# Fewer and larger on-chip transposes, casting loads from Pool's queue, and chunk extremes by trees, in a chunk-selecting attention with a gated feed-forward

## The chip, the core and the metric

The kernel runs on one core of one Trainium2 chip. The metric is the device time of one execution in microseconds (us). The profile's span of the same execution is about 2 us shorter than its device time. On one core an execution counts as fast unless it is over 1.5% above the fastest of the same kernel.

## The reference

There are 4 batches, 8 heads, 768 positions and 64 values per head. For each query the attention picks 6 of 24 chunks of 32 keys, by an upper bound made from each chunk's smallest and largest key, and attends only to those, causally. What comes out goes through a gated feed-forward layer of 512 to 1,536 to 512.

```python
k_chunks = k.reshape(B, H, nc, 32, D)
k_min, k_max = np.min(k_chunks, axis=3), np.max(k_chunks, axis=3)
ub = sum over d of maximum(q * k_min, q * k_max)      # one bound for each query and chunk
ub = np.where(causal, ub, -1e9)
top_chunks = np.argsort(ub, axis=-1)[..., -6:]
attn = softmax(scale * q @ k^T, only in top_chunks and causal) @ v
x = attn, heads side by side                           # (3072, 512)
out = (sigmoid(x @ w_gate) * (x @ w_val)) @ w_out
```

## The kernel before

The work is cut into eight units: batch 0 to 3, and the first (a) or second (b) 384 query rows. Unit 2b is the second half of batch 2. While TensorE computes the scores of one unit, the feed-forward of the unit before it is mixed in, and so is the preparation of the unit after it. Each engine's instructions stand in a fixed list; where an input came late, the engine stood in front of that instruction, and what was listed behind it waited too.

Data that needs its axes swapped is transposed by DMA, issued by SyncE. `hk` holds keys with the head dimension on the partitions, `hq` holds queries in the same way, with 32 rows below that mark chunks that were not selected, and `xT` holds the attention output for the feed-forward. Each of these is sent in pieces of one block of 128 rows:

```python
def keys_wide(u):                         # 3 transposes for each unit, 8 heads each
    nc.gpsimd.tensor_copy(kn16[u.half][:, :, :, 0:D], u.k)          # fp32 -> fp16
    for x in range(HB):                                              # HB = 3
        r = T * u.half + 128 * x
        nc.sync.dma_start_transpose(headK[u.b % 2][:, :, r:r + 128],
                                    kn16[u.half][:, x].rearrange("p h c -> p (h c)"))

def send_rows(u, j, x):                   # 6 for each unit, 4 heads each
    nc.sync.dma_start_transpose(headQ[u.half][:, 4 * j:4 * j + 4, 128 * x:128 * x + 128],
                                qn16[:, x, 4 * j:4 * j + 4].rearrange("p h c -> p (h c)"))

def turn(u, c):                           # 4 for each unit, 3 blocks each
    ...
    nc.sync.dma_start_transpose(u.xT[:, c, :].rearrange("p (x i) -> p x i", x=HB),
                                u.x[:, c].rearrange("p x d -> p (x d)"))
```

For each batch, chunk extremes come from a second load of the keys, in two spans of four heads (`kc`, 96 partitions = 4 heads x 24 chunks). VectorE reduces a strided view:

```python
def span_reduce(u, j, e):                 # e = 0: max, e = 1: min
    src = u.kc[j].rearrange("p s d -> p d s")
    for d0 in (0, 32):
        nc.vector.tensor_reduce(out=u.kmm[:, e, d0:d0 + 32], in_=src[:, d0:d0 + 32],
                                op=(ALU.max, ALU.min)[e], axis=AX.X)
```

Key, query and value blocks are loaded as fp32 by SyncE, and Pool casts keys and values to fp16 (`keys_wide` above, `cast_v`). Units 0a and 0b are prepared another way, in an opening that is written out by hand (`opening`).

The softmax here doesn't subtract the row's maximum and nothing guards it: scores larger than these inputs give would overflow.

Of the kernel before, what the change touches and what calls it, by code (L numbers as in the profile page):

```python
# [18 lines left out]
def kernel(  # L19
# [25 lines left out]
    loads = ctx.enter_context(tc.tile_pool(name="loads", bufs=2))  # L45
    kcp = ctx.enter_context(tc.tile_pool(name="kcp", bufs=1))
    loadv = ctx.enter_context(tc.tile_pool(name="loadv", bufs=1))
    sel = ctx.enter_context(tc.tile_pool(name="sel", bufs=1))
    ubp = ctx.enter_context(tc.tile_pool(name="ubp", bufs=2))
    attp = ctx.enter_context(tc.tile_pool(name="attp", bufs=3))  # L50
# [4 lines left out]
    hglp = ctx.enter_context(tc.tile_pool(name="hglp", bufs=15))  # L55
# [41 lines left out]
    def load_v(u):  # L97
        u.v = loadv.tile([128, HB, H, D], F32, tag="v", name=f"v_{u.name}")
        for i in range(HB):
            r = T * u.half + 128 * i  # L100
            nc.sync.dma_start(u.v[:, i], v[u.b, :, r:r + 128].rearrange("h p d -> p h d"))
# [6 lines left out]
    def load_block(u, n, i):  # L108
        src = {"k": k, "q": q, "v": v}[n]
        if i == 0:  # L110
            pool = loadv if n == "v" else loads
            tag = n if n == "v" else "raw" + n
            setattr(u, n, pool.tile([128, HB, H, D], F32, tag=tag, name=f"raw{n}_{u.name}"))
        r = T * u.half + 128 * i
        nc.sync.dma_start(getattr(u, n)[:, i], src[u.b, :, r:r + 128].rearrange("h p d -> p h d"))
# [5 lines left out]
    def load(u):  # L121
        for n, src in (("k", k), ("q", q)):
            t = loads.tile([128, H, HB, D], F32, tag="raw" + n, name=f"raw{n}_{u.name}")
# [6 lines left out]
    def regroup(u, n, parts):  # L130
        raw = getattr(u, "raw" + n)
        if not hasattr(u, n):
            setattr(u, n, (kn16[0] if n == "k" else qn16).bitcast(F32))
# [12 lines left out]
    qn16 = keep.tile([128, HB, H, 128], F16, tag="qn", name="qn")  # L146
    for i in range(2):
        kcat.append(keep.tile([128, H, 32], F32, tag=f"kcat{i}", name=f"kcat{i}"))
        headK.append(keep.tile([128, H, S], F16, tag=f"hk{i}", name=f"hk{i}"))
        kn16.append(keep.tile([128, HB, H, 128], F16, tag=f"kn{i}", name=f"kn{i}"))  # L150
        headQ.append(keep.tile([128, H, T], F16, tag=f"hq{i}", name=f"hq{i}"))
# [3 lines left out]
    def fill_pattern(i, eng):  # L155
        eng.dma_start(headK[i][64:96],
                      epat.rearrange("p c s -> p (c s)").unsqueeze(1).to_broadcast([32, H, S]))

    def constants():
# [6 lines left out]
        fill_pattern(0, nc.sync)  # L166
# [16 lines left out]
        nc.vector.memset(headQ[0][64:96, :, 0:128], 0.0)  # L183
        nc.vector.tensor_copy(ident16, ident32)

    def pattern_rows():
# [4 lines left out]
        nc.gpsimd.memset(qn16[:, :, :, 64:128], 0.0)  # L191
# [43 lines left out]
    def keys_f(u, p, eng):  # L235
        ps = u.kps.pop(p)
        for e in range(2):
            eng(headK[u.b % 2][0:64, 2 * p + e, u.rows], ps[64 * e:64 * e + 64])
# [34 lines left out]
    def queries_f(u, p, eng):  # L273
        ps = u.qps.pop(p)
        for e in range(2):
            eng(headQ[u.half][0:64, 2 * p + e, :], ps[64 * e:64 * e + 64])

    def keys_wide(u):
        nc.gpsimd.tensor_copy(kn16[u.half][:, :, :, 0:D], u.k)
        for x in range(HB):  # L280
            r = T * u.half + 128 * x
            nc.sync.dma_start_transpose(headK[u.b % 2][:, :, r:r + 128],
                                        kn16[u.half][:, x].rearrange("p h c -> p (h c)"))

    def span_reduce(u, j, e):
        if e == 0:
            u.kmm = sel.tile([96, 2, D], F32, tag="kmm", name=f"kmm_{u.name}_{j}")
        src = u.kc[j].rearrange("p s d -> p d s")
        for d0 in (0, 32):
            nc.vector.tensor_reduce(out=u.kmm[:, e, d0:d0 + 32], in_=src[:, d0:d0 + 32],  # L290
                                    op=(ALU.max, ALU.min)[e], axis=AX.X)
# [8 lines left out]
    def queries_wide(u):  # L300
        nc.gpsimd.tensor_copy(qn16[:, :, :, 0:D], u.q)
        if u.sel0:
            nc.gpsimd.memset(qn16[:, 0, :, 64:96], 0.0)
            first_rows(u, 0)

    def first_rows(u, x):
        for j in range(2):
            send_rows(u, j, x)

    def send_rows(u, j, x):  # L310
        nc.sync.dma_start_transpose(headQ[u.half][:, 4 * j:4 * j + 4, 128 * x:128 * x + 128],  # L311
                                    qn16[:, x, 4 * j:4 * j + 4].rearrange("p h c -> p (h c)"))
# [389 lines left out]
```

## Time and profile before

| | before |
|---|---|
| device time, median | 402.75 us (400.92 to 404.79, 4 runs) |
| span of the profiled execution | 398.7 us |
| TensorE (PE) busy, idle | 324.7 us, 74.0 us |
| mean granted clock of TensorE | 0.906 |
| VectorE (DVE), ScalarE (ACT), Pool busy | 180.3, 207.9, 79.5 us |

These are lines of the page of the kernel before: its span, the busy time of each engine, and two rows that cut the span into 40 slices of 10 us. A digit of the PE row is the busy share in tenths, and of the PEclk row the granted TensorE clock in tenths.

```profile
span 398.7 us, 6796 instructions
PE 324.7 (81%) x2547; PEld 195.7 (49%) x2547; DVE 180.3 (45%) x472; ACT 207.9 (52%) x441; POOL 79.5 (20%) x116
...
PE   5672778968697888959959796878988995999996
...
PEclk9867999996889696979978999696999999899999
```

No engine is full. TensorE is the busiest, and the dips in its PE row are followed by dips of its clock. The Trainium skill, "TensorE: Matmul & The Clock Gate" (Part 1, "What's actually happening"), says that the clock is halved after an idle window of about 3.4 us and released after a busy one. The trace agrees on the length: its clock records show twelve stretches at half clock, ten of 6.8 us and two of 3.4 us, nearly all just after a gap. Together they are 75.1 us, and half of that over the span of 398.7 us gives the missing 0.094.

The next lines are TensorE's waits. Each names the tile and line that waited, the engine and tile that ended the wait, the sum in us, the number of waits, and the longest.

```profile
PE xps_0a L415 <- DVE xT_0a L416: 5.9, 1, 5.9
PE kmT_1a L295 <- DVE kmm_1a L290: 5.2, 1, 5.2
...
PE v_0b L429 <- DVE hg_0b L432: 4.0, 1, 4.0
PE g_1b L423 <- DMA xT_1b<-xnat_1b: 3.9, 1, 3.9
PE g_2a L423 <- DMA xT_2a<-xnat_2a: 3.6, 1, 3.6
...
PE g_3a L423 <- DMA xT_3a<-xnat_3a: 3.1, 1, 3.1
PE sc_1b L378 <- DMA hq<-qn: 2.7, 1, 2.7
```

There are two families. TensorE waits for VectorE, which reduces chunks (`kmm`) or does what stands behind the reductions (`hg`, `xT_0a`). And it waits for transposes, `xT` and `hq`. The cost of one reduction, and the landing time of one query-row transpose, are in a group line of the same page and in a line of the view of DMA issues (mean ns of one instruction; median us from issue to landing):

```profile
L290 DVE TENSOR_REDUCE kmm_1a<-kc_1a 96x32 f32<-96x1024 f32 x8 | 14.6, 1864 | 6.2 <-DMA kc_1a<-in_k_dram 6.2
...
hq<-qn SPq DMA_TRANSPOSE x36, 2.5
```

How the transposes queue up is seen in the timeline of SyncE's queue at the boundary between units 3a and 3b (start us, duration us, what; a row may join several instructions):

```profile
326.58 3.82 SPq L311 DMA_TRANSPOSE hq<-qn  x3
330.49 0.53 SPq L443 DMA_DIRECT2D out_dram<-osb_2b  x1
331.13 3.86 SPq L311 DMA_TRANSPOSE hq<-qn  x3
335.08 0.54 SPq L443 DMA_DIRECT2D out_dram<-osb_2b  x1
335.71 1.21 SPq L410 DMA_TRANSPOSE xT_3a<-xnat_3a  x1
```

Six query-row transposes, at 1.27 us of issue each, stand ahead of the last `xT` copy of the unit before. TensorE waits 3.1 us for it (`g_3a` above).

In the opening, VectorE's timeline shows reductions ahead of the work that TensorE needs:

```profile
31.77 3.63 DVE L290 TENSOR_REDUCE kmm_1a<-kc_1a 96x32 f32<-96x1024 f32 x2 [1.32 <-DMA kc_1a<-in_k_dram]
35.32 0.18 DVE L402 RECIPROCAL rz_0a<-pv_0a 128x6 f32<-128x6 f32 x1
35.42 1.81 DVE L290 TENSOR_REDUCE kmm_1a<-kc_1a 96x32 f32<-96x1024 f32 x1
37.16 0.54 DVE L404 TENSOR_TENSOR xnat_0a<-pv_0a,rz_0a 128x384 f16<-128x384 f32 x1
```

TensorE stands for 5.9 us until 38.0 (`xps_0a` in the waits).

### The profile page before, as it was taken

The page shows a single profiled execution, that of the slowest core. Times are in us where ns is not written, and L with a number is a line of the kernel's source. Part 1 is how long each engine was busy: PE and PEld are TensorE (multiplying, and loading weights), DVE is VectorE, ACT ScalarE, POOL GpSimd, SP SyncE. Part 2 cuts the span into 40 slices and gives each one's busy share as a digit, 9 for nine tenths or more (in the row PEclk, how much of TensorE's full clock was granted, in tenths as well). Part 3 has the DMA queues.
Part 4 walks back from the last instruction along what each step waited for, and adds up shares of the span by engine and source line. Part 5 has one row for each costly group of instructions (what it writes and reads, how often), then busy time and mean ns, then how long its engine had stood idle before and what let it go on. Part 6 is the DMA issues. An engine that isn't in the chain of part 4 may idle for free. (4 is left out here: it accounts for less than half of the span.)

```text
span 398.7 us, 6796 instructions
## 1 busy us (share of the span) xinstructions
PE 324.7 (81%) x2547; PEld 195.7 (49%) x2547; DVE 180.3 (45%) x472; ACT 207.9 (52%) x441; POOL 79.5 (20%) x116
## 2 busy tenths in 40 slices
PE   5672778968697888959959796878988995999996
PEld 3361435535354445736535453555555553665552
DVE  6588547354435650393303772356323541431330
ACT  3670457657754224737537534465747634676331
POOL 3393003810051003201050113110114111011000
PEclk9867999996889696979978999696999999899999
DMA  8999990598439846796255956494437015001002
GB/s 223 265 223 193 196 207 2 96 224 185 91 67 191 159 76 144 153 134 117 77 115 118 216 80 127 95 195 109 100 94 111 12 49 128 12 12 56 36 2 79
DMA packets 125633, 47.54 MB, mean 119 GB/s; under 512 B 112992, under 2 KB 121952, under 8 KB 125024
## 3 DMA queue, kind: packets, MB, share of 16 engines
q1 hardware_dynamic: 120848, 42.39, 52.0%
q0 software_dynamic: 4752, 4.72, 7.0%
q8 instruction: 20, 0.33, 0.4%
q14 instruction: 13, 0.11, 0.1%
HBM read 33.03 MB, written 6.29 MB: 99 GB/s over the span
## 5 line engine op out<-in xcount | busy, mean ns | idle before, releaser
L429 PEld LDWEIGHTS <-wv 128*128 128x128 f16 x384 | 39.9, 104 | 55.8 <-issue 34.9
L378 PEld LDWEIGHTS <-hk 96*128 96x128 f16 x480 | 41.3, 105 | 33.5 <-issue 23.2
L423 PEld LDWEIGHTS <-wg 128*128 128x128 f16 x384 | 37.1, 103 | 25.8 <-issue 12.4
L381 ACT ACTIVATE att_1b<-sc_1b 128x512 f16<-128x512 f32 (+1 forms) x32 | 16.9, 574 | 7.4 <-PE sc_1b L378 7.2
L381 ACT ACTIVATE att_2b<-sc_2b 128x512 f16<-128x512 f32 (+1 forms) x32 | 16.8, 574 | 4.7 <-PE sc_2b L378 4.5
L381 ACT ACTIVATE att_3b<-sc_3b 128x512 f16<-128x512 f32 (+1 forms) x32 | 16.6, 570 | 5.0 <-PE sc_3b L378 4.7
L381 ACT ACTIVATE att_0b<-sc_0b 128x512 f16<-128x512 f32 (+1 forms) x32 | 16.6, 573 | 2.7 <-PE sc_0b L378 2.3
L290 DVE TENSOR_REDUCE kmm_1a<-kc_1a 96x32 f32<-96x1024 f32 x8 | 14.6, 1864 | 6.2 <-DMA kc_1a<-in_k_dram 6.2
L423 PE MATMUL g_2a<-xT_2a,wg 128*128 128x384 f16 x48 | 12.4, 367 | 6.1 <-DMA xT_2a<-xnat_2a 3.6
L290 DVE TENSOR_REDUCE kmm_3a<-kc_3a 96x32 f32<-96x1024 f32 x8 | 14.9, 1887 | 4.1 <-DMA kc_3a<-in_k_dram 4.1
L290 DVE TENSOR_REDUCE kmm_2a<-kc_2a 96x32 f32<-96x1024 f32 x8 | 14.8, 1866 | 4.5 <-DMA kc_2a<-in_k_dram 4.5
L432 DVE SCALAR_TENSOR_TENSOR hg_3a<-gate_3a,v_3a 128x384 f16<-128x384 f16 x12 | 6.7, 555 | 21.0 <-PE v_3a L429 10.1
L432 DVE SCALAR_TENSOR_TENSOR hg_2a<-gate_2a,v_2a 128x384 f16<-128x384 f16 x12 | 6.6, 551 | 20.3 <-ACT gate_2a L426 13.3
L429 PE MATMUL v_0b<-xT_0b,wv 128*128 128x384 f16 x48 | 11.8, 367 | 4.0 <-DVE hg_0b L432 4.0
L432 DVE SCALAR_TENSOR_TENSOR hg_1a<-gate_1a,v_1a 128x384 f16<-128x384 f16 x12 | 6.6, 549 | 18.7 <-ACT gate_1a L426 13.2
L378 PE MATMUL sc_1b<-hq,hk 96*128 96x128 f16 (+2 forms) x80 | 12.0, 274 | 3.2 <-DMA hq<-qn 2.7
L423 PE MATMUL g_1a<-xT_1a,wg 128*128 128x384 f16 x48 | 12.5, 369 | 2.6 <-DVE hg_1a L432 2.6
L384 POOL TENSOR_SCALAR_AFFINE_SELECT att_0b<-att_0b 128x384 f16<-128x384 f16 x8 | 4.1, 520 | 52.4 <-ACT att_0b L381 52.4
L423 PE MATMUL g_1b<-xT_1b,wg 128*128 128x384 f16 x48 | 11.3, 349 | 3.9 <-DMA xT_1b<-xnat_1b 3.9
L429 PE MATMUL v_0a<-xT_0a,wv 128*128 128x384 f16 x48 | 10.3, 339 | 4.4 <-ACT gate_0a L426 4.4
L423 PE MATMUL g_3a<-xT_3a,wg 128*128 128x384 f16 x48 | 11.2, 345 | 3.1 <-DMA xT_3a<-xnat_3a 3.1
L432 DVE SCALAR_TENSOR_TENSOR hg_0a<-gate_0a,v_0a 128x384 f16<-128x384 f16 x12 | 6.7, 554 | 15.5 <-ACT gate_0a L426 13.7
(286 smaller groups left out, 753.9 us busy)
## 6 DMA issues: line engine op xcount, KB each, us to landing
wg<-in_moe_w_gate_dram POOLq DMA_DIRECT2D x3, 512.0 KB, 11.5
wv<-in_moe_w_val_dram POOLq DMA_DIRECT2D x3, 512.0 KB, 14.1
kc_1a<-in_k_dram SPq DMA_DIRECT2D x2, 768.0 KB, 9.6
wo<-in_moe_w_out_dram POOLq DMA_DIRECT2D x3, 512.0 KB, 18.9
kc_2a<-in_k_dram SPq DMA_DIRECT2D x2, 768.0 KB, 5.8
kc_3a<-in_k_dram SPq DMA_DIRECT2D x2, 768.0 KB, 5.8
rawk_0a<-in_k_dram SPq DMA_DIRECT2D x2, 384.0 KB, 3.9
rawq_0a<-in_q_dram SPq DMA_DIRECT2D x2, 384.0 KB, 5.3
```

What stands on the lines that cost most here:

```text
L290: nc.vector.tensor_reduce(out=u.kmm[:, e, d0:d0 + 32], in_=src[:, d0:d0 + 32], op=(ALU.max, ALU.min)[e], axis=AX.X)
L378: nc.tensor.matmul(ps[:, o:o + w], headK[u.b % 2][0:96, h, 128 * jb:128 * jb + 128], headQ[u.half][0:96, h, i:i + w], start=True, stop=True)
L381: nc.scalar.activation(at[:, b0:b0 + n], ps, AF.Exp, scale=scale)
L384: nc.gpsimd.affine_select(out=dv, in_=dv, compare_op=ALU.is_ge, fill=0.0, base=0, pattern=[[0, HB], [1, 128]], channel_multiplier=-1)
L423: nc.tensor.matmul(gp, wg16[:, c, 128 * fb:128 * fb + 128], u.xT[:, c, :], start=(c == 0), stop=(c == 3))
L429: nc.tensor.matmul(vp, wv16[:, c, 128 * fb:128 * fb + 128], u.xT[:, c, :], start=(c == 0), stop=(c == 3))
L432: nc.vector.scalar_tensor_tensor(hg, gate, 1.0, vp, ALU.add, ALU.mult)
```

## The change

It means to take instructions off SyncE, the casts off Pool, and time off VectorE's chunk reductions.

1. **Merge.** `headK`, `headQ` and `qn16` are laid out by block of 128 rows, so that a unit sends its key rows in one transpose (24 blocks of 128 x 128), its query rows in two (12 blocks each) and `xT` in two (6 blocks each): 31 transposes on SyncE in the place of 81. In the last unit one more `xT` copy goes to TensorE, as the pairs leave two of four there.
2. **Loads.** Key and value blocks go to Pool's queue as casting loads straight into their fp16 tiles; query blocks go there too, still fp32. This removes Pool's casts of keys and values for units 1a to 3b; the queries are still cast there.
3. **Tree.** Chunk extremes by five elementwise maxima (or minima) over halves of the span, in the place of two strided reductions.
4. **Buffers.** One more buffer each for `att` and `hgl`. Units 0a and 0b share three raw buffers among keys, queries and values (before: two for keys, two for queries, one for values). The pattern under `headK[0]` is written in six pieces, three of them after the load of unit 0b, and not in one.

```diff
-    loads = ctx.enter_context(tc.tile_pool(name="loads", bufs=2))
+    loads = ctx.enter_context(tc.tile_pool(name="loads", bufs=3))
-    loadv = ctx.enter_context(tc.tile_pool(name="loadv", bufs=1))
-    attp = ctx.enter_context(tc.tile_pool(name="attp", bufs=3))
+    attp = ctx.enter_context(tc.tile_pool(name="attp", bufs=4))
-    hglp = ctx.enter_context(tc.tile_pool(name="hglp", bufs=15))
+    hglp = ctx.enter_context(tc.tile_pool(name="hglp", bufs=16))
... load_block: k and v into fp16 tiles, q into a raw tile
-        nc.sync.dma_start(getattr(u, n)[:, i], src[u.b, :, r:r + 128].rearrange("h p d -> p h d"))
+        nc.gpsimd.dma_start(dst, src[u.b, :, r:r + 128].rearrange("h p d -> p h d"))
... layouts
-    qn16 = keep.tile([128, HB, H, 128], F16, tag="qn", name="qn")
+    qn16 = keep.tile([128, 2, HB, 4, 128], F16, tag="qn", name="qn")
-        headK.append(keep.tile([128, H, S], F16, tag=f"hk{i}", name=f"hk{i}"))
+        headK.append(keep.tile([128, 2 * HB, H, 128], F16, tag=f"hk{i}", name=f"hk{i}"))
-        headQ.append(keep.tile([128, H, T], F16, tag=f"hq{i}", name=f"hq{i}"))
+        headQ.append(keep.tile([128, 2, HB, 4, 128], F16, tag=f"hq{i}", name=f"hq{i}"))
... keys_wide
-        nc.gpsimd.tensor_copy(kn16[u.half][:, :, :, 0:D], u.k)
-        for x in range(HB):
-            r = T * u.half + 128 * x
-            nc.sync.dma_start_transpose(headK[u.b % 2][:, :, r:r + 128],
-                                        kn16[u.half][:, x].rearrange("p h c -> p (h c)"))
+        nc.sync.dma_start_transpose(headK[u.b % 2][:, u.qa:u.qb].rearrange("p x h i -> p (x h) i"),
+                                    kn16[u.half].rearrange("p x h c -> p (x h c)"))
... span_reduce
-        src = u.kc[j].rearrange("p s d -> p d s")
-        for d0 in (0, 32):
-            nc.vector.tensor_reduce(out=u.kmm[:, e, d0:d0 + 32], in_=src[:, d0:d0 + 32],
-                                    op=(ALU.max, ALU.min)[e], axis=AX.X)
+        op = (ALU.max, ALU.min)[e]
+        src, n = u.kc[j], CH // 2
+        t = sel.tile([96, CH // 2, D], F32, tag="tree", name=f"tree_{u.name}_{j}_{e}")
+        while n >= 1:
+            dst = t[:, 0:n] if n > 1 else u.kmm[:, e:e + 1]
+            nc.vector.tensor_tensor(dst, src[:, 0:n], src[:, n:2 * n], op)
+            src, n = t, n // 2
... queries: the early send of the first 128 rows of an a unit (first_rows) goes, too
-    def send_rows(u, j, x):
-        nc.sync.dma_start_transpose(headQ[u.half][:, 4 * j:4 * j + 4, 128 * x:128 * x + 128],
-                                    qn16[:, x, 4 * j:4 * j + 4].rearrange("p h c -> p (h c)"))
+    def send_rows(u, j):
+        nc.sync.dma_start_transpose(headQ[u.half][:, j].rearrange("p x h i -> p (x h) i"),
+                                    qn16[:, j].rearrange("p x h c -> p (x h c)"))
... turn
-        if u is not units[0] and not (u is units[-1] and c == 3):
-            nc.sync.dma_start_transpose(u.xT[:, c, :].rearrange("p (x i) -> p x i", x=HB),
-                                        u.x[:, c].rearrange("p x d -> p (x d)"))
+        if u is not units[0] and not (u is units[-1] and c > 1):
+            if c % 2:
+                nc.sync.dma_start_transpose(
+                    u.xT[:, c - 1:c + 1, :].rearrange("p c (x i) -> p (c x) i", x=HB),
+                    u.x[:, c - 1:c + 1].rearrange("p c x d -> p (c x d)"))
... opening: the pattern under headK[0] in six pieces
         constants()          # writes the three pieces of unit 0a
         load(w)
+        fill_pattern(w)      # three pieces of unit 0b, behind its loads
```

Left out are the index changes that follow from the layouts, in the copies, in the matmuls of the scores and in the small fills.

More of the change, by code (lines that the diff above doesn't have):

```diff
@@ L97, in load_v @@
     def load_v(u):
-        u.v = loadv.tile([128, HB, H, D], F32, tag="v", name=f"v_{u.name}")
+        u.v = loads.tile([128, HB, H, D], F32, tag="raw", name=f"v_{u.name}")
         for i in range(HB):
@@ L109, in load_block @@
         src = {"k": k, "q": q, "v": v}[n]
-        if i == 0:
-            pool = loadv if n == "v" else loads
-            tag = n if n == "v" else "raw" + n
-            setattr(u, n, pool.tile([128, HB, H, D], F32, tag=tag, name=f"raw{n}_{u.name}"))
+        if n == "q":
+            if i == 0:
+                u.q = loads.tile([128, HB, H, D], F32, tag="raw", name=f"rawq_{u.name}")
+            dst = u.q[:, i]
+        elif n == "k":
+            dst = kn16[u.half][:, i, :, 0:D]
+        else:
+            dst = v16s[u.b % 2][:, u.qa + i, :, 0:D]
         r = T * u.half + 128 * i
-        nc.sync.dma_start(getattr(u, n)[:, i], src[u.b, :, r:r + 128].rearrange("h p d -> p h d"))
+        nc.gpsimd.dma_start(dst, src[u.b, :, r:r + 128].rearrange("h p d -> p h d"))
     def load_tasks(u):
@@ L122, in load @@
         for n, src in (("k", k), ("q", q)):
-            t = loads.tile([128, H, HB, D], F32, tag="raw" + n, name=f"raw{n}_{u.name}")
+            t = loads.tile([128, H, HB, D], F32, tag="raw", name=f"raw{n}_{u.name}")
             for j in range(2):
@@ L132, in regroup @@
         if not hasattr(u, n):
-            setattr(u, n, (kn16[0] if n == "k" else qn16).bitcast(F32))
+            t = kn16[0] if n == "k" else qn16.rearrange("p j x h c -> p (j x h) c").rearrange(
+                "p (x h) c -> p x h c", x=HB)
+            setattr(u, n, t.bitcast(F32))
         t = getattr(u, n)
@@ L145, with fill_pattern @@
     kcat, v16s, apt, headK, headQ, kn16 = [], [], [], [], [], []
-    qn16 = keep.tile([128, HB, H, 128], F16, tag="qn", name="qn")
+    qn16 = keep.tile([128, 2, HB, 4, 128], F16, tag="qn", name="qn")
     for i in range(2):
         kcat.append(keep.tile([128, H, 32], F32, tag=f"kcat{i}", name=f"kcat{i}"))
-        headK.append(keep.tile([128, H, S], F16, tag=f"hk{i}", name=f"hk{i}"))
+        headK.append(keep.tile([128, 2 * HB, H, 128], F16, tag=f"hk{i}", name=f"hk{i}"))
         kn16.append(keep.tile([128, HB, H, 128], F16, tag=f"kn{i}", name=f"kn{i}"))
-        headQ.append(keep.tile([128, H, T], F16, tag=f"hq{i}", name=f"hq{i}"))
+        headQ.append(keep.tile([128, 2, HB, 4, 128], F16, tag=f"hq{i}", name=f"hq{i}"))
         apt.append(keep.tile([128, HB, 4, 32], F16, tag=f"ap{i}", name=f"ap{i}"))
         v16s.append(keep.tile([128, 2 * HB, H, D + 1], F16, tag=f"v16{i}", name=f"v16{i}"))
-    def fill_pattern(i, eng):
-        eng.dma_start(headK[i][64:96],
-                      epat.rearrange("p c s -> p (c s)").unsqueeze(1).to_broadcast([32, H, S]))
+    def fill_pattern(u):
+        ep = epat.rearrange("p c s -> p (c s)")
+        for jb in range(u.qa, u.qb):
+            nc.sync.dma_start(headK[0][64:96, jb],
+                              ep[:, 128 * jb:128 * jb + 128].unsqueeze(1).to_broadcast([32, H, 128]))
     def constants():
@@ L165, in constants @@
         )
-        fill_pattern(0, nc.sync)
+        fill_pattern(units[0])
         nc.vector.memset(erow, NEG)
@@ L182, in constants @@
             nc.gpsimd.memset(v16s[i][:, :, :, D:D + 1], 1.0)
-        nc.vector.memset(headQ[0][64:96, :, 0:128], 0.0)
+        nc.vector.memset(headQ[0][64:96, :, 0], 0.0)
         nc.vector.tensor_copy(ident16, ident32)
@@ L190, in pattern_rows @@
             nc.gpsimd.memset(kn16[i][:, :, :, 96:128], 0.0)
-        nc.gpsimd.memset(qn16[:, :, :, 64:128], 0.0)
+        nc.gpsimd.memset(qn16[:, :, :, :, 64:128], 0.0)
     wg16 = keep.tile([128, 4, D_FF], F16, tag="wg16")
@@ L237, in keys_f @@
         for e in range(2):
-            eng(headK[u.b % 2][0:64, 2 * p + e, u.rows], ps[64 * e:64 * e + 64])
+            eng(headK[u.b % 2][0:64, u.qa:u.qb, 2 * p + e, :],
+                ps[64 * e:64 * e + 64].rearrange("p (x i) -> p x i", x=HB))
     def queries_t(u, p, pool, tag="ps"):
@@ L275, in queries_f @@
         for e in range(2):
-            eng(headQ[u.half][0:64, 2 * p + e, :], ps[64 * e:64 * e + 64])
+            eng(headQ[u.half][0:64, p // 2, :, 2 * (p % 2) + e, :],
+                ps[64 * e:64 * e + 64].rearrange("p (x i) -> p x i", x=HB))
     def keys_wide(u):
-        nc.gpsimd.tensor_copy(kn16[u.half][:, :, :, 0:D], u.k)
-        for x in range(HB):
-            r = T * u.half + 128 * x
-            nc.sync.dma_start_transpose(headK[u.b % 2][:, :, r:r + 128],
-                                        kn16[u.half][:, x].rearrange("p h c -> p (h c)"))
+        nc.sync.dma_start_transpose(headK[u.b % 2][:, u.qa:u.qb].rearrange("p x h i -> p (x h) i"),
+                                    kn16[u.half].rearrange("p x h c -> p (x h c)"))
     def span_reduce(u, j, e):
@@ L300, in queries_wide @@
     def queries_wide(u):
-        nc.gpsimd.tensor_copy(qn16[:, :, :, 0:D], u.q)
+        nc.gpsimd.tensor_copy(qn16[:, :, :, :, 0:D].rearrange("p j x h d -> p x j h d"),
+                              u.q.rearrange("p x (j h) d -> p x j h d", j=2))
         if u.sel0:
-            nc.gpsimd.memset(qn16[:, 0, :, 64:96], 0.0)
-            first_rows(u, 0)
-    def first_rows(u, x):
-        for j in range(2):
-            send_rows(u, j, x)
-    def send_rows(u, j, x):
-        nc.sync.dma_start_transpose(headQ[u.half][:, 4 * j:4 * j + 4, 128 * x:128 * x + 128],
-                                    qn16[:, x, 4 * j:4 * j + 4].rearrange("p h c -> p (h c)"))
+            nc.gpsimd.memset(qn16[:, :, 0, :, 64:96], 0.0)
+    def send_rows(u, j):
+        nc.sync.dma_start_transpose(headQ[u.half][:, j].rearrange("p x h i -> p (x h) i"),
+                                    qn16[:, j].rearrange("p x h c -> p (x h c)"))
     def queries_t_wide(u, p, pool, tag="ps"):
@@ L351, in pick @@
                 nc.vector.max(mx[:, x, h, :], ubm[:, x, h, :])
-        dst = qn16[:, u.sel0:HB, 4 * j:4 * j + 4, 64:64 + cb] if u.wide else apt[j][:, u.sel0:HB, :, 0:cb]
+        dst = qn16[:, j, u.sel0:HB, :, 64:64 + cb] if u.wide else apt[j][:, u.sel0:HB, :, 0:cb]
         nc.vector.tensor_tensor(dst, ubm,
@@ L355, in pick @@
         if u.wide:
-            for x in range(u.sel0, HB):
-                send_rows(u, j, x)
+            send_rows(u, j)
     def pick_t(u, j, eng):
@@ L365, in pick_t @@
         for i in range(4):
-            eng(headQ[u.half][64:96, 4 * j + i, s0:T], ps[32 * i:32 * i + 32, s0:T])
+            eng(headQ[u.half][64:96, j, u.sel0:HB, i, :],
+                ps[32 * i:32 * i + 32, s0:T].rearrange("p (x i) -> p x i", i=128))
     def score(u, h, x, pool=None, tag="ps"):
@@ L376, in score @@
         for (jb, i0, w) in u.banks[x]:
-            i = i0 - T * u.half
-            nc.tensor.matmul(ps[:, o:o + w], headK[u.b % 2][0:96, h, 128 * jb:128 * jb + 128],
-                             headQ[u.half][0:96, h, i:i + w], start=True, stop=True)
+            x0 = i0 // 128 - u.qa
+            nc.tensor.matmul(ps[:, o:o + w].rearrange("p (x i) -> p x i", i=128),
+                             headK[u.b % 2][0:96, jb, h, :],
+                             headQ[u.half][0:96, h // 4, x0:x0 + w // 128, h % 4, :], start=True, stop=True)
             o += w
@@ L454, in prep_wide @@
             r.append((0.0, pattern_rows))
-        r.append((0.0, lambda: (keys_wide(u), cast_v(u))))
+        r.append((0.0, lambda: keys_wide(u)))
         if u.half == 0:
```

## The prediction

> **What bounds it now.** One core, 403.05 us. By busy share TensorE leads: 324.7 of 398.7 us (81%); ACT 52%, DVE 45%, Pool 20%. What costs time is TensorE's 74 us of idling, and what follows it: the clock records hold about ten stretches of 6.8 us at half clock, nearly each after a TensorE gap of 2.5 to 6 us (mean granted clock 0.906). The Trainium skill, "TensorE: Matmul & The Clock Gate" (Part 1), describes this: the clock is halved after an idle window of about 3.4 us and released after a busy one; the trace agrees. So a removed gap saves itself and up to 3.4 us more.
>
> The gaps, from TensorE's waits and timeline:
> - 32-38 us: 5.9, DVE does chunk reductions (1.86 us each) ahead of xnat/xT.
> - 86-91: 5.2, second key span of 1a lands only at 83.9, then 7.3 us of reductions.
> - 127-131: 4.0 (hg_0b behind kc_2a); 171-177: 4.2; 267-273: 4.0: DVE waiting for kc and reducing.
> - 102-107: 3.2, ACT's signs of 1b.
> - 148-151: 2.75, hq of 1b: SyncE spends 3.8 us on three transposes, a 1.7 us store, three more.
> - 204-207, 247-250, 335-338: 3.9, 3.6, 3.1: last xT, behind transposes and a store.
>
> **What the change does.**
> 1. SyncE: 81 transposes at 1.2-1.3 us of issue become 31. Issue hardly depends on size (3 blocks 1.2, 8 blocks 1.33), so I take 1.5-1.8 us for 24. Landing grows 2.5 us (4 blocks) to 3.3 (8): estimated 4.1 for 12, 6.5 for 24, 2.8 for xT pairs. Three issues and the last landing (5.0 us) become about 4.1. More important: kc is issued 2.5 us earlier, without k/q/v blocks around it.
> 2. Nine k/q/v blocks per unit go to Pool's queue. A weight load of 512 rows took Pool 0.75 us; 1,024 rows per block: estimate 1.0-1.5. 54 blocks add 55-80 us of Pool, 17.6 us of casts leave (12 x 1.46). Pool rises to 115-145 us, not the bound, but up to five blocks stand ahead of a causal select, which can hold it 5 us; about one head period is slack. Estimated cost: 3-8 us. That casting loads must come from Pool is in the skill's "DMA: Bandwidth & Descriptors" (SWDGE vs HWDGE); the weight loads do so here.
> 3. Tree: 1,984 fp32 outputs at about 1.04 ns plus five times 0.15 us (from the 288- and 384-element tensor_tensors) is 2.8 us against two reductions, 3.73. About 11 us less DVE over 12. More comes from order: in the built order the first trees stand behind all four xT copies, and hg steps slip between tree levels.
> 4. One more att and hgl buffer; units 0/1 share three raw buffers: small.
>
> **On the critical path.** The five DVE/kc gaps mostly vanish (about 18 of 23 us), 102-107 and 148-151 shrink (about 4), xT gaps stay (1 less). Warm clock: six of ten cold stretches gone, about 15 us where TensorE binds. Against that 5-8 us of new select and landing waits. A check: 3a, a first-half unit without loads or trees beside it, takes 36 us against 44 and 48 of 2a and 1a.
>
> **Prediction: 373 us, 360 to 392 (8 in 10).** Faster by over 2%: 0.87; within 2%: 0.09; slower: 0.04.
>
> **Right if** TensorE no longer waits for kmm or for hg behind kmm; mean clock about 0.94; tree levels sum to 2.7-3.1 us; a send-rows issue under 1.6 us; Pool busy 115-145 us; waits for hq under 1 us each. **Wrong if** a Pool load issue takes 2 us or more, so that pv waits for selects; merged transposes' issue or landing grows in proportion to blocks; casting 128 B writes slow the queues so that kc still lands late; or the gaps merely move, and the clock stays at 0.90.

## The result, and the profile after

| | before | after |
|---|---|---|
| device time, median | 402.75 us (400.92 to 404.79, 4 runs) | 368.35 us (363.89 to 369.56, 4 runs) |
| ratio | | 0.911 [0.901, 0.920] |
| span of the profiled execution | 398.7 us | 366.7 us |
| TensorE busy, idle | 324.7, 74.0 us | 312.7, 54.0 us |
| mean granted clock | 0.906 | 0.941 |
| TensorE waiting for `xT` | 12.1 us | 6.8 us |
| TensorE waiting for `hq` | 7.2 us | 3.7 us |
| TensorE waiting for VectorE's `kmm`, `hg`, `xT`, `xnat` | 25.9 us | 15.5 us |
| DVE, ACT, Pool busy | 180.3, 207.9, 79.5 us | 172.0, 207.3, 112.7 us |

A ratio is the mean time of one kernel's fast runs over that of the other's of the same rounds, with a 95% interval, so it is not quite the ratio of the medians. One of the four runs after (369.56 us) counts as slow; it is in the median and not in the ratio. The three rows of waits add up the lines of TensorE's waits by what was waited for.

The result is inside the predicted range, 4.65 us below the predicted time. The lines of the page after that answer to those of before:

```profile
span 366.7 us, 6742 instructions
PE 312.7 (85%) x2550; PEld 190.2 (52%) x2550; DVE 172.0 (47%) x509; ACT 207.3 (57%) x441; POOL 112.7 (31%) x158
...
PE   4687178887859997989969997989989999999995
...
PEclk9958679998999999889998999899999999999998
```

The span fell by 32.0 us: 20.0 us less idle time, and 12.0 us less busy time for the same matmuls, because the clock was higher: of TensorE's busy time 59.5 us lay inside half-clock stretches before and 33.8 us after, and half of the difference is 12.9 us. The half-clock stretches in the clock records add up to 43.2 us in the place of 75.1, and from about 80 us on none is longer than 3.4 us. The exception is the fifth slice of the PE row (37 to 46 us, as a slice is 9.2 us here): it is 1, and the fourth before (30 to 40 us) was 2, so this dip has not gone.

TensorE's waits after:

```profile
PE g_0a L431 <- DVE hg_0a L440: 8.3, 1, 8.3
...
PE sc_0b L383 <- DVE xnat_0b L410: 3.3, 1, 3.3
PE g_2a L431 <- DMA xT_2a<-xnat_2a: 2.3, 1, 2.3
PE g_1a L431 <- DMA xT_1a<-xnat_1a: 1.9, 1, 1.9
PE g_1b L431 <- DMA xT_1b<-xnat_1b: 1.9, 1, 1.9
...
PE kmT_2a L304 <- DVE kmm_2a L299: 1.4, 1, 1.4
```

The `xT` waits of the later units are shorter, the waits behind reductions have nearly gone, and at the head there is a new wait of 8.3 us. SyncE's timeline at the same boundary between 3a and 3b shows why `xT` comes sooner:

```profile
298.84 1.43 SPq L316 DMA_TRANSPOSE hq<-qn  x1
300.37 0.83 SPq L451 DMA_DIRECT2D out_dram<-osb_2b  x1
301.89 1.42 SPq L316 DMA_TRANSPOSE hq<-qn  x1
303.41 0.89 SPq L451 DMA_DIRECT2D out_dram<-osb_2b  x1
304.39 1.26 SPq L417 DMA_TRANSPOSE xT_3a<-xnat_3a  x1
```

A transpose of 12 blocks is issued in 1.43 us here and three of 4 blocks in 3.82. The last `xT` copy goes out 5.55 us after the first send, not 9.13, and the wait for it fell from 3.1 to 0.4 us.

Next, two lines of the view of one source line, for the tree's first and last level (count; minimum, median and maximum ns; first and last start):

```profile
L299 DVE TENSOR_TENSOR tree_1a<-kc_1a x4: 1221/1222/1222, 41.9 to 85.6; 96x1024 f32<-96x1024 f32 x4
...
L299 DVE TENSOR_TENSOR kmm_1a<-tree_1a x4: 210/221/222, 45.9 to 88.6; 96x64 f32<-96x64 f32 x4
```

The five levels take 1.22, 0.69, 0.42, 0.29 and 0.22 us, so a tree takes 2.83 us where two reductions took 3.73. The Trainium skill, "VectorE: DVE Perf Modes" (the section on the TRN2 errata of SBUF-source operations), gives (N + 151)/0.96 ns for an fp32 `tensor_tensor` of N elements, which makes an estimate of 1,224 ns for the first level and 2.85 us for all five. The trace agrees (1,222 ns and 2.83 us).

For the kernel after, the group line of Pool's issues of key blocks (from its page) and the line of the query rows (from the view of DMA issues):

```profile
L118 POOL DMA_DIRECT2D kn<-in_k_dram x18 | 16.0, 896 | 0.3 <-issue 0.3
...
hq<-qn SPq DMA_TRANSPOSE x12, 3.8
```

A block costs Pool 0.90 us, and 12 blocks of query rows land 3.8 us after their issue (4 blocks took 2.5).

The new wait in the opening is seen in the timeline of VectorE:

```profile
31.72 0.36 DVE L424 COPY xT_0a<-xps_0a 128x384 f16<-128x384 f16 x1 [0.90 <-PE xps_0a L423]
32.00 1.01 DVE L233 TENSOR_REDUCE kmx<-kT_0b 128x12 f32<-128x384 f32 x2
41.88 1.22 DVE L299 TENSOR_TENSOR tree_1a<-kc_1a 96x1024 f32<-96x1024 f32 x1 [8.88 <-DMA kc_1a<-in_k_dram]
43.14 0.69 DVE L299 TENSOR_TENSOR tree_1a<-tree_1a 96x512 f32<-96x512 f32 x1
43.75 0.55 DVE L440 SCALAR_TENSOR_TENSOR hg_0a<-gate_0a,v_0a 128x384 f16<-128x384 f16 x1
```

And this is the timeline of SyncE's queue some time before it:

```profile
15.13 7.33 SPq L100 DMA_DIRECT2D v_0b<-in_v_dram  x3
22.51 5.22 SPq L163 DMA_DIRECT2D hk<-epat  x3
27.77 0.60 SPq L104 DMA_DIRECT2D kc_1a<-in_k_dram  x1
```

The copies of `xT_0a` now stand ahead of the trees, as predicted, so TensorE's gap before 38 us is gone. But the first key span of 1a was issued at 27.77 us, not at 18.21 as before, and landed at 41.9. In front of it on SyncE stand the query and value loads of 0b and three pieces of the pattern. The value loads were through at 22.5 us and not at 18.2 as before (the query loads, which now share the raw buffers, went out at 14.17 and not at 11.03), which is 4.3 us of the 9.6; the pieces are the other 5.3. How much of the 4.3 is the buffers was not tested. VectorE stood 8.88 us in front of its first tree, with an `hg_0a` behind it that TensorE needed.

The starts of the scores of each unit tell which stages gained (us in the profile; the last column is from the start of 0b to the end):

| kernel | 0b | 1a | 1b | 2a | 2b | 3a | 3b | span | 0b to end |
|---|---|---|---|---|---|---|---|---|---|
| before | 64.8 | 100.6 | 148.0 | 198.6 | 242.0 | 294.3 | 330.0 | 398.7 | 333.9 |
| after | 66.4 | 106.5 | 140.6 | 187.6 | 223.6 | 269.9 | 302.6 | 366.7 | 300.3 |

The opening lost 1.6 us, and all of the gain, 33.6 us, came later.

### The profile page after: what moved, and what is told of

Read it like the earlier page. It is cut to its first block, busy times and chain, and to the rows that moved or that the text cites. A ratio compares the mean times of both kernels' runs of the same rounds, so it can differ in the third digit from the quotient of the medians.

```text
span 366.7 us, 6742 instructions
## 1 busy us (share of the span) xinstructions
PE 312.7 (85%) x2550; PEld 190.2 (52%) x2550; DVE 172.0 (47%) x509; ACT 207.3 (57%) x441; POOL 112.7 (31%) x158
## 5 line engine op out<-in xcount | busy, mean ns | idle before, releaser
L383 PEld LDWEIGHTS <-hk 96*128 96x128 f16 x480 | 39.3, 102 | 29.5 <-issue 15.8
L431 PE MATMUL g_0a<-xT_0a,wg 128*128 128x384 f16 x48 | 11.8, 358 | 8.3 <-DVE hg_0a L440 8.3
L387 ACT ACTIVATE att_3b<-sc_3b 128x512 f16<-128x512 f32 (+1 forms) x32 | 16.6, 570 | 3.8 <-PE sc_3b L383 3.6
L118 POOL DMA_DIRECT2D v<-in_v_dram x18 | 16.0, 904 | 3.9 <-DMA wo<-in_moe_w_out_dram 3.4
L118 POOL DMA_DIRECT2D kn<-in_k_dram x18 | 16.0, 896 | 0.3 <-issue 0.3
L383 PE MATMUL sc_0b<-hq,hk 96*128 96x128 f16 (+2 forms) x80 | 11.4, 255 | 3.9 <-DVE xnat_0b L410 3.3
L390 POOL TENSOR_SCALAR_AFFINE_SELECT att_3b<-att_3b 128x384 f16<-128x384 f16 x8 | 4.2, 522 | 31.9 <-ACT att_3b L387 31.9
L437 PE MATMUL v_0a<-xT_0a,wv 128*128 128x384 f16 x48 | 10.4, 341 | 4.0 <-ACT gate_0a L434 4.0
L390 POOL TENSOR_SCALAR_AFFINE_SELECT att_3a<-att_3a 128x384 f16<-128x384 f16 x8 | 4.2, 522 | 30.3 <-ACT att_3a L387 30.3
L390 POOL TENSOR_SCALAR_AFFINE_SELECT att_2b<-att_2b 128x384 f16<-128x384 f16 x8 | 4.5, 568 | 29.1 <-ACT att_2b L387 29.1
L390 POOL TENSOR_SCALAR_AFFINE_SELECT att_1b<-att_1b 128x384 f16<-128x384 f16 x8 | 4.3, 542 | 29.8 <-ACT att_1b L387 29.8
L245 ACT CAST hk<-kT_0b 64x384 f16<-64x384 f32 x8 | 3.8, 474 | 16.7 <-DVE kmx L233 15.0
L440 DVE SCALAR_TENSOR_TENSOR hg_1a<-gate_1a,v_1a 128x384 f16<-128x384 f16 x12 | 6.6, 551 | 13.7 <-PE v_1a L437 9.8
## 6 DMA issues: line engine op xcount, KB each, us to landing
kc_1a<-in_k_dram SPq DMA_DIRECT2D x2, 768.0 KB, 10.8
```

Of the source, the lines that this page charges most:

```text
L118: nc.gpsimd.dma_start(dst, src[u.b, :, r:r + 128].rearrange("h p d -> p h d"))
L245: eng(headK[u.b % 2][0:64, u.qa:u.qb, 2 * p + e, :], ps[64 * e:64 * e + 64].rearrange("p (x i) -> p x i", x=HB))
L383: nc.tensor.matmul(ps[:, o:o + w].rearrange("p (x i) -> p x i", i=128), headK[u.b % 2][0:96, jb, h, :], headQ[u.half][0:96, h // 4, x0:x0 ...
L387: nc.scalar.activation(at[:, b0:b0 + n], ps, AF.Exp, scale=scale)
L390: nc.gpsimd.affine_select(out=dv, in_=dv, compare_op=ALU.is_ge, fill=0.0, base=0, pattern=[[0, HB], [1, 128]], channel_multiplier=-1)
L431: nc.tensor.matmul(gp, wg16[:, c, 128 * fb:128 * fb + 128], u.xT[:, c, :], start=(c == 0), stop=(c == 3))
```

## The experiments

The theory after the result: the gain is a sum of the three parts, and the largest is not the tree or the loads but the merge, because SyncE's queue at the unit boundaries holds up `hq` and `xT`. One rival: most of it comes from VectorE's gaps (tree and earlier `kc`), as the prediction's sum had it. Another: the extra buffers do it. And for the opening: the late key span, against a cost that belongs to the tree itself.

All kernels below gave correct results. The runs came in three sets, each on another chip, with the kernel before beside them; the control was run in the first set alone. Medians and ranges are of all runs, slow ones too; ratios are of fast runs. The profile of a_open2_again is of its slow execution. The median of the kernel before beside these runs was 402.84 to 405.33 us.

| label | kernel | median us (range) | ratio to before | profiled span, clock |
|---|---|---|---|---|
| after_again | the changed kernel, as a control | 365.89 (364.64 to 368.42) | 0.904 [0.900, 0.909] | 366.7, 0.936 |
| a_split | changed, all transposes split again | 389.07 (385.55 to 389.22) | 0.959 [0.954, 0.964] | 383.9, 0.938 |
| a_hqsplit2 | changed, only the query rows split | 382.95 (382.37 to 385.68) | 0.953 [0.945, 0.960] | 380.7, 0.933 |
| a_hkxtsplit | changed, key rows and xT split | 371.24 (369.89 to 375.30) | 0.924 [0.917, 0.931] | 368.2, 0.937 |
| a_notree | changed, reductions for trees | 380.74 (377.31 to 386.53) | 0.941 [0.936, 0.946] | 375.6, 0.949 |
| a_bufs | changed, old number of att and hgl buffers | 364.03 (360.39 to 365.62) | 0.898 [0.892, 0.903] | 363.9, 0.948 |
| b_pool2 | before, only the Pool loads added | 396.77 (393.59 to 398.44) | 0.985 [0.974, 0.995] | 394.9, 0.914 |
| b_merge2 | before, only the merge added | 386.33 (386.03 to 388.33) | 0.961 [0.954, 0.967] | 384.8, 0.929 |
| a_open22 | changed, first key span of 1a earlier | 362.50 (356.88 to 363.19) | no interval | 355.2, 0.952 |
| a_open2_again | the same, more rounds | 359.14 (358.04 to 363.86) | 0.892 [0.887, 0.897] | 362.2, 0.953 |
| a_open2_bufs | the same, and old buffer numbers | 360.48 (358.59 to 362.98) | 0.895 [0.890, 0.900] | 359.1, 0.952 |
| a_open2_kc_bufs | that, and the second key span earlier | 365.77 (364.52 to 367.53) | 0.909 [0.904, 0.914] | 365.8, 0.930 |

TensorE's waits by class in the profiled executions (us; sums of the lines of its waits):

| kernel | for xT | for hq | for VectorE's kmm, hg, xT, xnat |
|---|---|---|---|
| before | 12.1 | 7.2 | 25.9 |
| after_again | 6.3 | 3.6 | 17.8 |
| a_split | 15.8 | 9.1 | 15.5 |
| a_hqsplit2 | 14.8 | 9.9 | 15.7 |
| a_hkxtsplit | 6.2 | 4.7 | 17.6 |
| a_notree | 6.0 | 4.9 | 23.2 |
| b_pool2 | 15.3 | 9.6 | 27.4 |
| b_merge2 | 4.3 | 2.8 | 34.4 |
| a_open2_bufs | 7.0 | 3.6 | 8.3 |

### The changed kernel again (after_again)

No edit; it is the control for the runs beside it.

> The changed kernel unaltered, as a control on this chip. Both theories: 364 to 371 us, ratio 0.905 to 0.920.

It gave 365.89 us and a ratio of 0.904, just under the range written down, with an interval that overlaps that of the first measurement. Differences to the changed kernel below are taken to this median.

### All transposes split again (a_split)

```diff
 def keys_wide(u):
-    nc.sync.dma_start_transpose(headK[u.b % 2][:, u.qa:u.qb]..., kn16[u.half]...)
+    for x in range(HB):
+        nc.sync.dma_start_transpose(headK[u.b % 2][:, u.qa + x],
+                                    kn16[u.half][:, x].rearrange("p h c -> p (h c)"))
 ... queries_wide: for a units, send_rows(u, 0, 0) and send_rows(u, 1, 0) early, as in the kernel before
-def send_rows(u, j):
+def send_rows(u, j, x):
+    nc.sync.dma_start_transpose(headQ[u.half][:, j, x], qn16[:, j, x].rearrange("p h c -> p (h c)"))
 ... turn: one transpose for each c
```

> Changed kernel with its transposes split per row block again, loads from Pool, trees and buffers kept. Theory 1 (the gain comes from TensorE gaps behind key spans and chunk extremes, freed by moving loads and by the trees): the merge is worth little, 371 to 377 us; the three key transposes take SyncE about 4 us as the one did (3.6 to 4.3 us), only hq sends cost it 2.4 us more each. Theory 2 (the merge is the main part): most of the gain is lost, 385 us or more.

It gave 389.07 us, 23.2 us above the changed kernel. Loads, tree, layouts and buffers are as in the changed kernel, so this is what the merge is worth on top of the rest. The waits say where: `xT` 15.8 us and `hq` 9.1, somewhat more than in the kernel before, while the waits for VectorE did not grow. In the profiles, 15.2 of the 17.2 us between the control and this kernel are idle time of TensorE and 2.0 are busy time; this profile is of the fastest run, 3.5 us under the median.

### Only the query rows split (a_hqsplit2), and its complement (a_hkxtsplit)

The edit of the first is the `queries_wide` and `send_rows` part of the diff above; of the second, the `keys_wide` and `turn` parts.

> Changed kernel with only the query rows' transposes (hq) split again, keys' and xT transposes merged. If the merge's worth is SyncE's time between the picks and the last xT (3.8 us instead of 1.4 per send): most of the split's 20 us comes back, 380 to 388 us, and waits for xT and hq as in the full split. If it is the keys' or the xT merge, no more than 373 us.

> The changed kernel with the key-row transposes in three pieces and the xT copies one by one, but the query rows merged: the complement of the run that splits only the query rows (382.95 us, 17 us above the changed kernel's 366). All three split cost 23 us (389.07). Theory A (the parts add): this costs 23 - 17 = 6 us, so 369 to 374, and almost all of the merge's worth sits in the query rows, because their merged form also lets the stores and xT through sooner. Theory B (the three stand in one SyncE queue and any one lengthens the boundary between units, so the parts overlap): 10 us or more, 376 to 385, with waits for xT of the middle units back at 2.5 to 4 us each as in the fully split run.

They gave 382.95 us (17.1 above the control) and 371.24 us (5.4 above). The parts add in medians: 17.1 + 5.4 = 22.5, against 23.2 for both. As the sets differ, the ratios are the safer measure: 4.8 and 2.0 points above the control, against 5.4 for both, which is the same picture with more scatter. So some 71 to 76% of the two is the query rows, and only in part because scores wait for query rows: with query rows split and `xT` still merged, the waits for `hq` rise by 6.3 us over the control, but those for `xT` by more, 8.5 us to 14.8, while splitting `xT` itself leaves them at 6.2. The `xT` copies are late because of what stands ahead of them in SyncE's queue. The timeline of that queue in a_hqsplit2, at the boundary between 3a and 3b:

```profile
305.49 3.81 SPq L318 DMA_TRANSPOSE hq<-qn  x3
309.40 0.52 SPq L454 DMA_DIRECT2D out_dram<-osb_2b  x1
310.03 3.85 SPq L318 DMA_TRANSPOSE hq<-qn  x3
313.98 0.53 SPq L454 DMA_DIRECT2D out_dram<-osb_2b  x1
314.60 2.51 SPq L420 DMA_TRANSPOSE xT_3a<-xnat_3a  x1
```

The transpose of `xT_3a` goes out 9.11 us after the first send, as in the kernel before (9.13), and TensorE waited 4.5 us for it.

### The tree undone (a_notree)

```diff
-    ... five nc.vector.tensor_tensor over halves
+    src = u.kc[j].rearrange("p s d -> p d s")
+    for d0 in (0, 32):
+        nc.vector.tensor_reduce(out=u.kmm[:, e, d0:d0 + 32], in_=src[:, d0:d0 + 32],
+                                op=(ALU.max, ALU.min)[e], axis=AX.X)
```

> Changed kernel with the two tensor_reduce per extreme instead of the max tree, everything else kept. Theory 1: DVE busy rises by about 9 to 11 us, TensorE's waits for kmm and for hg behind it come back in part (3 to 6 us, with some half-clock stretches): 374 to 382 us. Theory 2: DVE is not the bound, no more than 371 us.

It gave 380.74 us, 14.9 above the control; the profiled execution alone is 8.9 us longer, and the range of this kernel's runs is wide (the profiled one had the highest clock of the five, 0.949 against 0.911 to 0.940). VectorE's busy time is 180.9 us, 9 more than in the changed kernel. The waits for VectorE grow from 17.8 to 23.2 us, with `kmT_1a` at 6.3, `kmT_2a` at 3.2 and `kmT_3a` at 2.9. The tree is a real part of the gain, but the smaller one beside the merge.

### Buffer numbers put back (a_bufs)

```diff
-    attp = ... bufs=4        +    attp = ... bufs=3
-    hglp = ... bufs=16       +    hglp = ... bufs=15
```

> Changed kernel with three att and fifteen hgl buffers as before. Theory 1 and 2: within 1% of the changed kernel, 366 to 372 us. Theory 3 (the extra buffers let scores run ahead of the causal selects that the loads on Pool delay): 376 us or more, and TensorE waits for att.

It gave 364.03 us, 1.9 below the control, with overlapping intervals. No worth of these buffers shows.

### Only the Pool loads (b_pool2), and only the merge (b_merge2), on the kernel before

The first takes the `load_block` part of the change and drops the two casts. The second takes the layouts and all merged transposes, but loads and reduces as before, and writes the six pattern pieces up front.

> The kernel before with only the keys, queries and values of the wide units loaded by Pool's queue (cast into the fp16 tiles), split transposes, reductions and its own buffers kept. Theory 1 (loads leaving SyncE's queue bring the key spans earlier and are a large part): 385 to 392 us, kc waits of DVE fall below 2 us each. Theory 4 (the parts add, and the first four runs leave only some 3 us for the loads): 395 to 402 us.

> The kernel before with only the merged transposes (and their tile layout); loads on SyncE, reductions and buffers as before (the pattern in six pieces at the start). Theory 4 (the parts add; the merge is worth about 20 us by shortening the hq sends and what waits behind them, the last xT): 378 to 388 us, TensorE's waits for xT fall from 12 to about 7 us. Theory 1 (merge small): 392 us or more.

The loads alone gave 6.1 us (402.88 to 396.77). The waits for `xT` and `hq` stayed (15.3 and 9.6 us), and so did those for VectorE, because the reductions in the opening still stand ahead of the `xT_0a` copies. VectorE's waits for `kc` did not fall below 2 us as theory 1 had it: they were 9.1, 4.2 and 2.5 us for 1a, 2a and 3a, against 6.2, 4.5 and 4.1. The loads were not taken out of the changed kernel.

The merge alone gave 16.6 us (402.88 to 386.33), although it lost much at the start: its scores of 0b begin at 76.9 us, 12.1 later than before, behind a wait of TensorE for `xT_0a` that grew from 5.9 to 16.6 us. Its first key span went out at 29.01 us, behind six pattern pieces and the loads of 0b, and VectorE stood 12.32 us for it: the trouble of the changed kernel's opening again. After that start it is 26.0 us faster than the kernel before (307.9 against 333.9), and the loads alone 7.5 us (326.4). Of the 26.0 us, 13.7 are busy time of TensorE and 12.4 idle time. It has the smallest waits for `xT` and `hq` of all these kernels. So the merge, not the loads, removes those waits, whether it is added to the old kernel or taken out of the new one.

Added to what the tree is worth, the single parts come to 6.1 + 16.6 + 14.9 = 37.6 us, near the 37.0 to 39.4 us between the control and the medians of the kernel before. This sum mixes parts added to the old kernel with one taken out of the new one; a run with the tree alone was not made.

### The first key span of 1a earlier (a_open22, a_open2_again)

```diff
 def load_tasks(u):
-    return ([lambda: load_span(u, 0)] if u.half == 0 else []) + r
+    return ([lambda: load_span(u, 0)] if u.half == 0 and u is not units[2] else []) + r
 def load(u):
         ...
         setattr(u, "raw" + n, t)
+        if n == "k" and u is units[1]:
+            load_span(units[2], 0)       # right behind the keys of 0b
```

> Changed kernel with the first key span of 1a loaded right behind the keys of 0b instead of behind its values and the pattern. If the 8 to 11 us gap of the opening is DVE standing in the first tree for a span that lands at 41.9 us: the gap vanishes or falls below 3 us, 356 to 362 us. If the opening is bound by DMA bandwidth, the wait only moves to xnat or the weights and the time stays within 1% of the changed kernel.

> The early load of the second pair's first key span once more, because its first three rounds had one execution at 356.9 us and three at 362.4 to 363.2, and so gave no interval. Expected: median 360 to 363, ratio to the kernel before 0.89 to 0.90, against 0.904 for the changed kernel; the low one was the clock (0.952 against 0.943 to 0.948). If the ratio comes out above 0.902 the opening's gap is not worth what its 6 us in the profile say.

In SyncE's queue of a_open22 the span now goes out at 11.52 us:

```profile
10.38 1.10 SPq L128 DMA_DIRECT2D rawk_0b<-in_k_dram  x2
11.52 0.50 SPq L104 DMA_DIRECT2D kc_1a<-in_k_dram  x1
```

Its first tree starts at 24.58 us, the wait of TensorE for `hg_0a` is gone, and the scores of 0b begin at 59.9 us, against 66.4 and 67.7 in the two profiles of the changed kernel. This profile is of the fast outlier of the series; in a_open2_again's profile, of a slow run, they begin at 63.3. The first series has no interval: one execution took 356.9 us and the other three 362.4 to 363.2, over 1.5% above it, so they were counted as slow. With more rounds the median is 359.14 us and the ratio 0.892 [0.887, 0.897], apart from the control's [0.900, 0.909]. So the 8.3 us wait belongs to the late load, not to the tree, and it cost the changed kernel 5 to 7 us (1.2 points of the ratio; 6.8 us between medians). What was written down about the low execution did not hold: the two profiled executions of this kernel, with spans of 355.2 and 362.2 us, had the same clock (0.952 and 0.953). Of the 7.0 us, 3.4 had arisen by the start of 0b's scores; beyond that the spread stays unexplained.

### The two together, and the second key span earlier (a_open2_bufs, a_open2_kc_bufs)

The first joins the last edit with the old buffer numbers. The second also issues the second key span of 1a, 2a and 3a ahead of the merged key-row transpose, behind which it stood.

> Two of the variants together: the first key span of the second pair loaded right behind the first pair's keys (measured alone: 362.5 us, 355.2 profiled at a lucky 0.952 clock), and the number of att and hgl buffers put back (measured alone: 364.03 us, within 0.7% of the changed kernel). If the opening is what the changed kernel loses and the extra buffers are worth nothing: ratio to the kernel before 0.885 to 0.90, 357 to 363 us, scores starting at about 60 us in the profile and not at 66 to 68, and no TensorE gap above 2 us before that. If the earlier run's profile was luck of the clock: 364 or more.

> As the variant with the early first span and the old buffer counts, and the second key span of 1a, 2a, 3a issued ahead of the merged key-row transpose. In the changed kernel it lands behind that transpose (median landing of the first such load 10.8 us, at about 82 us) and holds scores of 0b (xnat wait 3.3 us). Theory A: that wait goes, 2 to 4 us faster than without (355 to 360). Theory B: the early tree is taken up by DVE before the span landed, DVE stands, and what stands behind it (xnat, xT, hg) loses as much: same or slower, a DVE wait for kc of over 10 us in the profile.

The first gave 360.48 us, the same as without the buffer edit within the intervals. The second was slower, 365.77 us. One line of VectorE's timeline in that run says why:

```profile
48.05 1.22 DVE L301 TENSOR_TENSOR tree_1a<-kc_1a 96x1024 f32<-96x1024 f32 x1 [7.08 <-DMA kc_1a<-in_k_dram]
```

The tree of this second span was put into VectorE's list early as well. VectorE stood there for 7.08 us until the span had landed, and TensorE's wait for `hg_0a` was back (6.8 us). That is the rival theory of this run, though its wait was 7.1 us and not the over 10 that was written down. The wait for `xnat_0b` behind the second span did go, but more was lost than that.

The best version is thus the changed kernel with the early first span: 359.14 us, 10.8% under the kernel before and about 1.3% under the changed kernel (0.892 against 0.904).

## Why the prediction was right, and where its steps were off

The time (373 predicted, 368.35 and 365.89 measured), the mechanism (gaps of TensorE and the half clock behind them) and the mean clock (about 0.94; 0.941 and 0.936 measured) were right. Within the sum, errors in both directions nearly cancelled, so that the total came so close is in part luck.

| step | predicted | measured |
|---|---|---|
| tree, five levels | 2.7 to 3.1 us | 2.83 us |
| issue of a query-row transpose | under 1.6 us | 1.43 us in the median; 9 of 12 under 1.6, three 1.91 to 2.54 |
| landing of 12 blocks | 4.1 us | 3.8 us |
| issue of 24 blocks | 1.5 to 1.8 us | 3.6 to 4.3 us |
| landing of 24 blocks | 6.5 us | 5.8 us |
| landing of an xT pair | 2.8 us | 2.6 us for 3a, but 4.7 to 5.9 us for 1a to 2b |
| Pool issue for one block | 1.0 to 1.5 us | 0.9 us |
| Pool busy | 115 to 145 us | 112.7 us |
| saved by a higher clock | about 15 us | 12.0 us less TensorE busy time |
| saved in VectorE and kc gaps | about 18 us | 10.4 us (25.9 to 15.5) |
| saved in the xT gaps | 1 us | 5.3 us (12.1 to 6.8) |
| saved at 102-107 and 148-151 | about 4 us | 3.8 us (`qs_1b` 3.2 to 1.8, `hq` of `sc_1b` 2.7 to 0.3) |
| new waits for selects and landings | 5 to 8 us | for selects none (2.0 to 0.7 us) |

- **"xT gaps stay (1 less)" failed.** The prediction counted the issue time of the `xT` copies themselves. What mattered more was the six query-row transposes ahead of them in the same queue: merged, they let `xT` go out 3.6 us sooner at the 3a/3b boundary, and a_hqsplit2 brought the waits for `xT` back to 14.8 us without touching `xT`. The merge as a whole was undervalued: its removal costs 23.2 us.
- **"The five DVE/kc gaps mostly vanish (about 18 of 23 us)" was over-sized.** After the opening they did, down to waits for `kmm` of 1.2 to 1.4 us. In the opening the gap at 32-38 moved to 36-44 and grew from 5.9 to 8.3 us. The order of instructions was read correctly (the trees stand behind the `xT_0a` copies), but not when their input would land. Three more pattern pieces in front (5.3 us) and later query and value loads of 0b, which now share raw buffers with the keys (4.3 us), put the key span 9.6 us later in SyncE's queue. The prediction had passed over the buffers as "small" and had not named the pieces. The early-span runs show that the late span cost 5 to 7 us. The prediction's first test, that TensorE no longer waits for `kmm` or for `hg` behind it, was thus missed: 8.3 us for `hg_0a`, behind the first tree.
- **"5-8 us of new select and landing waits" did not come.** Pool's loads were issued in 0.9 us each and Pool had time to spare. The one new landing wait is 3.3 us for `xnat_0b`, behind the second key span of 1a, whose SyncE issue came after the 4.25 us issue of the merged key rows.
- **The issue of 24 blocks was mis-sized.** "Issue hardly depends on size" held from 3 to 12 blocks (1.2 to 1.43 us) and broke at 24: 3.6 to 4.3 us, 3.95 in the mean, against 4.35 for three sends of 8 in the profile before. That is growth about in proportion to the blocks, which the prediction had put under "wrong if"; for the key rows it came true and cost little. This is in line with the small worth of the key-row and `xT` merges (5.4 us together).
- **Two more of its tests were missed narrowly.** Two waits for `hq` were 1.1 us each, not under 1, and Pool's 112.7 us are just under the range.
- **The loads** were given no number of their own for the critical path, and the loads alone gave 6.1 us. That casting loads have to come from Pool, as the Trainium skill says in "DMA: Bandwidth & Descriptors" ("SWDGE vs HWDGE vs iDMA"), no run here tests; all casting loads did come from Pool's queue.

What stays open: how much of the merge is the shorter waits themselves and how much is the clock behind them differs with the kernel. In the profiles after the start of 0b, TensorE's busy time makes up 13.7 of 26.0 us where the merge was added, but 2.5 of 20.6 us where it was taken out (control against a_split). No run separates the pattern pieces from the shared raw buffers. The worth of the tree is between 8.9 us (one profile) and 14.9 us (medians).

## What to carry to other kernels

Before valuing a merged transfer, look at what stands behind it in the same queue at the point where the critical engine waits: here six small sends cost TensorE more in waits for the copy queued after them (8.5 us) than in waits for themselves (6.3 us). When a change reorders buffers and fills in an opening, follow each load to its issue and landing as well as each instruction to its place, since here an engine that reached an instruction before its data had come held up what was listed behind it (VectorE, 8.88 us). Test a part both by adding it to the old kernel and by taking it out of the new one; for the merge, the only part tested both ways, they agreed (16.6 us added, 23.2 taken out).

## What the Trainium skill lacked or had wrong

- "DMA: Bandwidth & Descriptors" ("DMA Transpose (X-bar)") has no time measured on this chip for the issue on the queue by size. Measured on SyncE: mostly 1.2 to 1.35 us for 3 to 8 blocks of 128 x 128 fp16 from SBUF to SBUF, 1.43 us in the median for 12 (1.27 to 2.54), but 3.6 to 4.3 us for 24. Landing took 2.5 us for 4 blocks, 3.3 for 8, 3.8 for 12 and 5.8 for 24 (medians).
- The same page ("SWDGE vs HWDGE vs iDMA") says who may cast but gives no figure for what the issue costs Pool: 0.90 us for each block of 1,024 rows of 64 values, which landed in about 5 us (4.7 for keys, 5.4 for values).
- "VectorE: DVE Perf Modes" (the tier table) gives `tensor_reduce` one rate and no time for a strided input. With a strided view in SBUF as input, 1,024 fp32 elements took 1.86 us (1.82 ns for each). Over a contiguous view (in PSUM), 384 took about 0.55 us, and the first level of the tree, with 1,024 outputs, took 1.22 us.
- "TensorE: Matmul & The Clock Gate" (Part 1, "What's actually happening") has the clock halved after an idle window of about 3.4 us. The half-clock stretches here last multiples of 3.4 us, which agrees, but windows that were not idle led to them too: in the 3.4 us before the twelve stretches of the kernel before, TensorE was busy for 7 to 51%.
